# A gated mix of two long convolutions: the short filter as matmuls on a transposed load, and Q rows made for two blocks at a time

## The chip, the core and the metric

The kernel runs on one core of one Trainium2 chip. The metric is the device time of one execution in microseconds. Three runs of the kernel before took 285.6, 288.29 and 289.53 us, so its time is the median, 288.29 us. One more execution was profiled; its span, from the first to the last recorded instruction, is 282.3 us.

## What is computed

There are L = 2048 time steps, D = 448 channels and N = 256 modes per channel. All inputs are bf16, and `A_ref` and `B_ref` are the two convolution branches.

```python
# A: the kernel of the convolution is a sum over the modes of a channel
dt = exp(log_dt)[:, None]; A = A_re + 1j*A_im; Bc = B_re + 1j*B_im; Cc = C_re + 1j*C_im
P = exp((dt*A)[:, :, None] * arange(L))
K = einsum("dn,dnl,dn->dl", Cc, P, dt*Bc).real
y_a = causal_conv(u, K) + u * Dskip              # the reference uses FFTs of length 2L
# B: a short filter over k, then a long convolution
k_shift[t] = sum(k[t - 3 + i] * shift_k[:, i] for i in range(4))   # zeros before t = 0
kv = k_shift * v
y_b = u * (causal_conv(kv, ssm_k) + kv * ssm_D)
# mix
g = sigmoid((u * gate_w).sum(-1, keepdims=True))
out = g * y_a + (1 - g) * y_b
```

## The kernel before

**Layout.** Time is split as 32 x 64 and the channels into four groups of 112. A tile such as `vt` or `uu` holds 128 partitions (group g at 32g, the coarse time a on the 32 partitions within it) by 64 fine steps b by 112 channels. The 448 channels are worked in four chunks H of 28 columns (NQG, NC), which are 112 channels of the four groups.

**Convolution by matmuls.** Both sides of a convolution are brought into the frequency domain by two steps: `spread` (L311, psum tiles `ps_c`, matrix `Wc`) and `transform` (L323, `ps`, `s_W`). ACT evacuates both into tiles `zs` (inputs) or `zsK` (the generated K). `swapped` (L703) makes a copy `zsS` with the real and the imaginary half exchanged, by two DMAs from SP. `products` (L385) multiplies by the other side on DVE. Then come `stage_a` (L360, `ps_a`, matrix `sa_R`, evacuated into `U`) and `stage_b` (L373, `ps_b`, matrix `sb_G`), whose results an epilogue multiplies by u and gathers in `ug`.

**K generated in blocks.** K is made in eight blocks j (two to a chunk H) by `KGen` (L392). `Tables.levels` (L576) makes the powers of the modes for a chunk, two blocks at once: phases `ks_ph` on DVE, sines and exponentials on ACT into `ET`. In a block DVE builds 25 complex Q rows (`kg_TQ`, two buffers, M = 112 modes wide) and 32 P rows (`kg_TP`): `mult` makes products into `kg_P`, `add` sums them, and `leaf` writes products that need no sum (rows 17 to 24). Then PE runs 224 small matmuls `pk`: 25 columns of `kg_TQ` as weights, a strided view of `kg_TP` as the moving side. ACT evacuates `pk` into `kg_S`; `gather` (L475) sorts it by matmuls (`ps_g`) into `kg_KT`, which is spread with `WcK` into `zsK`, in groups of 4, 4, 3 and 3 columns, or 7 and 7 for the last two blocks. `step` (L893) ties a block j to the stages of one convolution, in the order of `seq`.

**The short filter.** 16 DMAs on SP load k into `kt` (L720), in pieces of 112 KB whose rows are 224 bytes. One shifting matmul (`ps_h`) fills the three steps before each row of 64. For eight fine steps at a time (L758 to 768) DVE multiplies a window of k by the four taps (`kvt`, 3584 elements), eight matmuls with the identity add the four products up (`ps_v`), and ACT evacuates into `kt`. Four DVE products with `vt` give `kv`.

**Set-up.** Six loads bring the modes (224 KB each). `wide` transposes them on PE (`ps_m`, 48 pieces), and `scaled` (L526) multiplies by dt on DVE. `Consts.stage_b` (L234) makes G by 16 sines on ACT with a mask in the scale (`sb_G`).

**Order.** Every call is recorded by the class `Order` (L132) and issued in the order of the list `ORDER` (L41), which fixes the order on each engine; the tile framework adds the semaphores and the pools make an instruction wait for its buffer. PSUM has three tiles of two banks (`psum`), one for `pk`, and one for `ps_g`; `qp` has NBQ = 8 buffers. All instructions are issued from L144, so that the profile's rows name this one line, and a reader goes by the names of the tiles.

Of the kernel before, what the change touches and what calls it, by code (L numbers as in the profile page):

```python
# [17 lines left out]
P = 128  # L18
# [13 lines left out]
NQ = 25  # L32
# [5 lines left out]
NBQ = 8  # L38
# [3 lines left out]
    "604 2 1 188 173 582 190 160 194 73 186 19 0 174 192 187 74 534 22 576 5 189 75 593 526 583 9 525 11 3 606 177 4 "  # L42
    "30 26 25 23 67 528 552 161 536 550 18 8 21 597 544 166 16 49 32 198 175 171 542 69 33 191 38 76 535 176 13 529 "
    "196 172 577 537 179 543 580 602 178 12 162 195 181-182 527 193 553 197 65 15 163 201 184 545 588 594 183 589-590 "
    "202 72 20 6 46 24 540 14 70 31 29 538 532 34 27-28 35 37 36 40 44 42 51 66 39 41 45 79 180 541 539 531 77 "
    "234-241 52 43 50 47-48 199 56 68 242 78 164 168 595 100-108 533 215-222 603 200 167 591 581 185 530 90 109 592 "
    "120-128 598 110-118 546 129 548 547 223 551 150 224 140 130 225-232 169 233 203-204 119 151-159 549 243-260 557 "
    "556 554 131-139 555 503 80 205-212 599 165 17 10 7 499 213 474 170 478 494 482 214 517 262 507 578 516 584 513 "
    "481 585 493 476 498 469 477 486 512 508 141-149 91-98 475 99 468 267 285-301 471-473 261 81-89 55 54 53 367 "
    "364-365 487 319-326 366 489 502 327 268-283 302-317 284 318 607 490 263 600 346-354 495 504 518 264 505 837-844 "  # L50
    "421-428 519 479 586 509 500 62 61 63 514 337-345 265 596 587 601 501 491 579 488 483-484 506 515 1124 1126 "
    "370-386 429 558 521 564-565 266 520 1127 570 845 560 64 608-635 574-575 71 636-663 522 1129 523 510 524 480 1131 "
    "496 1137 563 485 566 664-719 470 720 803-818 1133 571 567 561 721-722 819 1138 492 1135 497 568 573 511 404-420 "
    "1113 387-402 1114-1115 1140 1116 1142 1109 2488 569 562 1117 1122 1119 1118 57 59 786-801 1110 559 802 572 "
    "820-836 2492 2491 355-362 1852 1121 403 430-437 2494 363 457-464 328-335 438 465 336 439-446 2497 1108 60 58 "
    "448-455 1111-1112 2489 447 1464-1479 1498-1513 2503 1480 2496 456 1851 1123 1853 1143 1125 1854 1128 1855 723 "
    "1130 1856 1132 2514 1859 1120 1134 605 777-784 2490 1141 1136 2515 1514-1522 1139 1144-1175 2495 1523 1860 2502 "
    "2504 1857-1858 2516 726-741 368 1272-1303 1861 1176-1207 785 742 760-776 2510 1862 743-758 960-967 2519-2520 759 "
    "2521 369 466 1208-1239 2511 467 1863 969-976 2512-2513 968 977 1304-1367 1240-1271 1368 2508 2507 2498 1864-1865 "
    "2499 2517 933-941 1867 2509 863-879 725 1869 2523 2505 1369-1386 2500 1481-1496 2524-2525 1871 2501 1866 1497 "  # L60
    "2542 2533-2534 2543 1868 1873 2544 1879 880-896 2535 2506 906-914 1644-1651 846-861 1387-1426 1652 2518 1427 "
    "915-931 862 932 2537-2538 2545 1875 1878 2539 1876 1880 2562-2563 2529 1870 2564 1872 2526 1874 2528 2565 1877 "
    "1881 897-905 942-949 1847 1461 1446-1451 1662-1670 950 2530 2557 1452 1075-1106 2551 2566 3331 2531-2532 "
    "978-1074 2554 1671-1679 2558 2553 2546 2074-2105 1882-1913 2567 2536 2570 1107 2572 2568 2540 1946-1977 1848 "
    "2547 1849 2219-2234 2559 2571 2550 2235 2493 2522 2569 2574 1453-1459 2010-2041 951-959 1653-1660 2552 2549 2541 "
    "2548 1978-2009 1460 1463 2555 2561 2527 2573 2202-2217 1437-1445 1846 1850 2966-2981 2042-2073 2982 2556 2560 "
    "1914-1945 1661 3332 2218 2575 1428-1436 2106 3968 2236-2252 3974 2576 3333 1462 1584-1600 1618-1633 3971 "
    "1635-1642 2107-2123 1643 3975 3977 3970 2124 1634 1601-1616 1524-1540 2125-2164 1575-1582 2165 3334 1583 1617 "
    "3976 1541-1556 2175-2183 3969 2253-2261 1557-1574 3973 2349-2356 2578 3335 2580 2577 2949-2964 1716-1747 2357 "
    "3338 3982 2579 3972 2582 2586 3983 2584 2587 2581 3336 2583 2590 2965 3339 2589 3340 2591 3341 2585 3343 2592 "  # L70
    "1698-1706 3337 3346 2588 1748-1779 3995 3348 2184-2189 1680-1687 3984 1780 3342 3350 3985 3352 2190 2593-2624 "
    "1707-1714 1688 2657-2688 1715 3994 3354 4008 3357 2785-2816 4009 6194 1689-1697 2199 2625-2656 2166-2174 "
    "2322-2330 4010 2340-2347 2198 2200-2201 2983-2998 2191-2197 2753-2784 2999 2721-2752 3000-3008 3996 2689-2720 "
    "2920-2928 3344 3978 3156-3164 2929-2936 3345 3988 3347 3979-3980 3349 3987 3351 3989 2262-2277 4022 2937 2278 "
    "4004 3981 4011 4003 4023 3355 2348 3353 4005 1813-1844 2331-2338 4024 3358 3999 4025 4006 4017 4043 2339 "
    "2313-2320 1781-1812 2321 2817 4012 3986 3060-3068 4018-4019 4000 3356 1845 3991 2818-2834 3990 4042 3360 4044 "
    "4001 3138-3146 2835 2296-2311 3992 2312 4002 4045 4013-4014 2279-2294 4020 2295 3043-3059 4015 2836-2875 3993 "
    "4046 2876 3997-3998 3359 3361 4032 4027 2390-2421 2423-2454 4047 4016 4048 4034-4035 4031 4028 4037 2358-2389 "
    "4050 4049 2422 3426-3457 4052 4051 4007 4053 4041 4021 3554-3585 4030 4033 4038 3490-3521 2895-2900 4040 "
    "2938-2946 4026 2901 2455-2486 3458-3489 3394-3425 2487 4029 4036 4054 3522-3553 3733-3740 3362-3393 2911-2918 "  # L80
    "4055 4039 3741 4057 3699-3714 2902-2907 2919 3009-3024 2908 3715 3025 2886-2894 5388 4056 5393 3026-3042 4059 "
    "4058 4812 4060 4811 4061 4813 4063 4062 4066 4064 5402 4069 3147-3155 3716-3732 5391 3586 2877-2885 5392 "
    "4070-4071 4067 2909-2910 2947-2948 4814 5396 3682-3697 3183-3190 3698 5399 4815 4065 3587-3604 4446-4461 4816 "
    "4072 3174-3181 3605-3644 3191 4819 4462 5394 3645 4068 3192-3200 5395 3646-3653 3182 3129-3137 5389 3120-3127 "
    "5390 3654 3128 4820 5398 5400 3103-3119 4821 5403 4822 5404 4823 5411 5410 5412 3811-3819 4073-4104 4265-4296 "
    "3802-3810 4233-4264 4826 4818 4817 5415 5414 5413 5420 4828 4137-4168 3655-3663 5416 3069-3084 5401 4830 "
    "4169-4232 4105-4136 5419 4297 4825 3165-3173 3671-3677 4824 4832 5421 4827 4834 4829 5407-5409 3664-3669 3085 "
    "3670 4831 5443 5442 4833 4837 3086-3102 5424 5423 4835 724 5445 5444 4749-4765 4400-4408 5422 5437 5425 "
    "4463-4479 4391-4398 4838 4399 3201-3232 4316-4356 4418-4426 5438 5463 4836 3829-3837 4840 4839 5429 5428 5430 "
    "5405-5406 4298-4315 5439 4841 5426 5434 5417-5418 5433 5435 5431-5432 5462 3678-3679 3681 3680 5464 3820-3828 "  # L90
    "4390 4480-4487 4389 5427 5460 5473 4488 3233-3264 5002-5033 4874-4905 4938-4969 4906-4937 4842-4873 3298-3329 "
    "3266-3297 3330 4970-5001 5034-5065 5456 5449 5448 3265 5465 5458 3793-3800 4366-4373 5397 3801 3742-3758 5447 "
    "4715-4731 5459 4409-4417 3776-3792 3759-3774 4374 3775 4732-4748 4357-4364 4766-4774 5436 5466 6200 5467 5476 "
    "5850 5470 5849 5471-5472 5475 5474 5851 5450 5440-5441 4427-4428 5468 5478 5477 5480 4365 5479 3838-3902 5446 "
    "5486 5481 4775-4783 4429-4445 4540-4548 5487 5483 5469 4375-4381 5454 4506-4521 5461 5457 5066 3903-3934 "
    "4382-4388 4523-4538 5455 4522 5067-5084 5452 4539 5451 5453 5852 3935-3967 4558-4565 5085-5125 4489-4505 "
    "4802-4809 5482 5853 5484-5485 5489 5151-5157 5490-5491 4566 5488 5492-5556 5589-5620 5854 5144-5150 6197 "
    "5857-5859 4576-4583 4810 5685-5716 5653-5684 5126-5134 4567-4575 5557-5588 5621-5652 5717 4584 5855 5860 5856 "
    "5861 5863-5864 5862 5866 5865 5868 5867 5870 5869 5873 5871 5874 5876 5135-5142 4549-4556 5143 5872 5878 4557 "
    "5158 5877 5879 4585-4649 5160-5168 4784-4791 5718-5735 5178-5185 4792 5186 5159 5169-5176 5736-5776 5177 "  # L100
    "4682-4713 4650-4681 4714 5875 5187-5197 5792-5805 4793-4801 5808 5806 5777-5791 5880-5975 6203 5807 6198 6195 "
# [894 lines left out]
```

## Time and profile before

| | us |
|---|---|
| runs | 285.6, 288.29, 289.53 |
| span of the profiled execution | 282.3 |
| the profiled execution's own time around its span | not given by the profile |
| end of the first kg_S evacuation | 83.8 |
| end of the last kg_S evacuation | 250.8 |

A row of a group names line, engine, operation, output and inputs with their shape and count; behind the bar stand the busy time of all in us and the mean of one in ns, and behind the second bar the idle time of the engine just before them and what ended it. A piece of the timeline has its start, its length and how many instructions it holds. "PEld" are the weight loads of PE. The clock in a row of windows is the share of full speed that was granted to PE. In the slices of the page a digit is the busy share of 1/40 of the span in tenths.

### The profile page before, as it was taken

What the parts mean: (1) busy time and instruction counts of PE and PEld (TensorE: products, weight loads), DVE (VectorE), ACT (ScalarE), POOL (GpSimd) and SP (SyncE); (2) the same over time, 40 slices, a digit from 0 to 9 for tenths busy, and PEclk for the clock granted to TensorE, in tenths of its full rate; (3) what the DMA queues carried; (4) which work ended last, traced back from release to release, by engine and by line L of the source; (5) the groups of instructions that cost most, each with busy time, mean ns of one, the idle gap of its engine ahead of it and who ended that gap; (6) DMA issues with size and microseconds to landing.
All of it is one profiled execution on the core that took longest, in us unless ns stands there. A gap on an engine that the chain in (4) does not pass through costs nothing.

```text
span 282.3 us, 12050 instructions
## 1 busy us (share of the span) xinstructions
PE 213.7 (76%) x5387; PEld 185.9 (66%) x5387; DVE 261.8 (93%) x540; ACT 250.8 (89%) x409; POOL 12.0 (4%) x43
## 2 busy tenths in 40 slices
PE   0187673776697869888889898879899999979730
PEld 0044243776586768877779787868789887869730
DVE  8999999999999997999999999999968999987950
ACT  5999999999999999999999999999979999948500
POOL 8005000001000001000000000000000000000000
PEclk9999797565888997999999997988979999979995
DMA  6999997590501360240000070015050003430068
GB/s 116 190 182 176 158 168 105 187 175 6 135 2 19 69 115 10 73 107 2 5 2 5 6 181 0 5 22 114 9 128 2 2 5 73 112 88 5 2 126 138
DMA packets 53380, 21.34 MB, mean 76 GB/s; under 512 B 48720, under 2 KB 51664, under 8 KB 53328
## 3 DMA queue, kind: packets, MB, share of 16 engines
q1 hardware_dynamic: 48768, 19.42, 37.2%
q10 hardware_dynamic: 4560, 1.15, 2.2%
q8 instruction: 42, 0.69, 1.1%
q14 instruction: 10, 0.08, 0.1%
HBM read 10.01 MB, written 3.21 MB: 47 GB/s over the span
## 4 chain that ended last, share of the span: by engine, by line
ACT 34%; DVE 30%; PE 21%; issue 5%; DMA 3%; SPq 2%; DVEq 0%
ACT zs L144 11%; PE pk L144 8%; ACT ET L144 8%; DVE kg_P L144 7%; DVE kg_TP L144 5%; PE ps_b L144 4%; ACT zsK L144 4%; ACT U L144 4%; DVE zsS L144 3%; PE ps_c L144 3%; PE ps_a L144 3%; DVE kg_TQ L144 3%; DVE zs L144 2%; DVE kvt L144 2%; DVE ks_ph L144 2%
## 5 line engine op out<-in xcount | busy, mean ns | idle before, releaser
L144 ACT CAST zs<-ps 128x896 bf16<-128x896 f32 x48 | 44.0, 940 | 0.8 <-PE ps L144 0.7
L144 ACT CAST zs<-ps_c 128x1024 bf16<-128x1024 f32 (+1 forms) x48 | 43.4, 933 | 0.0
L144 PE MATMUL pk<-kg_TP,kg_TQ 128*25 128x32 bf16 x1792 | 33.8, 239 | 8.8 <-issue 6.6
L144 PEld LDWEIGHTS <-s_W 128*128 128x128 bf16 x544 | 31.0, 105 | 12.1 <-issue 8.7
L144 PEld LDWEIGHTS <-kg_TQ 128*25 128x25 bf16 x1792 | 28.6, 128 | 12.2 <-issue 8.2
L144 PE MATMUL ps_a<-sa_R,zs 128*128 128x128 bf16 x224 | 34.1, 239 | 3.0 <-ACT zs L144 1.3
L144 DVE TENSOR_TENSOR kg_P<-kg_TQ,ET 128x896 bf16<-128x896 bf16 (+2 forms) x56 | 35.9, 654 | 0.0
L144 PE MATMUL ps<-zs,s_W 128*128 128x112 bf16 x384 | 29.3, 231 | 7.3 <-ACT zs L144 6.2
L144 PE MATMUL ps_a<-sa_R,zsS 128*128 128x128 bf16 x224 | 33.7, 239 | 1.2 <-DVE zsS L144 1.2
L144 PEld LDWEIGHTS <-zsS 128*128 128x128 bf16 x224 | 30.1, 153 | 4.9 <-issue 3.0
L144 ACT CAST U<-ps_a 128x1024 bf16<-128x1024 f32 (+2 forms) x30 | 28.6, 959 | 5.0 <-PE ps_a L144 5.0
L144 PE MATMUL ps_b<-U,sb_G 128*128 128x28 bf16 x1024 | 28.8, 174 | 3.4 <-DVE U L144 1.2
L144 PEld LDWEIGHTS <-zs 128*128 128x128 bf16 x224 | 30.2, 152 | 1.3 <-issue 0.3
L144 PEld LDWEIGHTS <-sb_G 128*128 128x128 bf16 x1024 | 27.8, 96 | 4.3 <-issue 2.3
L144 DVE TENSOR_TENSOR kg_P<-kg_TP,ET 128x1792 bf16<-128x1792 bf16 (+1 forms) x32 | 30.6, 969 | 0.0
L144 DVE TENSOR_TENSOR kg_TQ<-kg_P 128x448 bf16<-128x448 bf16 (+2 forms) x56 | 23.1, 419 | 0.0
L144 PEld LDWEIGHTS <-scratch 128*128 128x128 bf16 x65 | 6.8, 109 | 24.6 <-issue 19.7
L144 ACT ACTIVATE ET<-ks_ph 128x448 bf16<-128x448 int16 x40 | 22.5, 604 | 0.0
L144 ACT CAST zsK<-ps_c 128x384 bf16<-128x384 f32 (+2 forms) x27 | 21.3, 797 | 0.6 <-PE ps_c L144 0.6
L144 DVE TENSOR_TENSOR kg_TP<-kg_P 128x896 bf16<-128x896 bf16 (+2 forms) x40 | 19.7, 503 | 0.2 <-PE pk L144 0.2
L144 PE MATMUL ps_c<-Wc,kv 128*64 128x128 bf16 x224 | 16.6, 303 | 3.9 <-ACT zs L144 3.6
L144 PE MATMUL ps_v<-kvt,scratch 128*128 128x448 bf16 x64 | 16.1, 405 | 4.0 <-ACT kt L144 3.2
(103 smaller groups left out, 463.3 us busy)
## 6 DMA issues: line engine op xcount, KB each, us to landing
zsS<-zs SPq DMA_DIRECT2D x16, 448.0 KB, 5.7
kt<-in_B_k_dram SPq DMA_DIRECT2D x16, 112.0 KB, 4.0
skraw<-in_B_ssm_k_dram SPq DMA_DIRECT2D x16, 112.0 KB, 5.0
vt<-in_B_v_dram SPq DMA_DIRECT2D x4, 448.0 KB, 7.7
uu<-in_A_u_dram SPq DMA_DIRECT2D x4, 448.0 KB, 8.8
xfd<-ks_hold SPq DMA_DIRECT2D x2, 672.0 KB, 3.2
ks_xf<-xfd SPq DMA_DIRECT2D x3, 336.0 KB, 3.7
out_dram<-ug SPq DMA_DIRECT2D x8, 112.0 KB, 4.0
```

Source lines behind the costliest of these rows:

```text
L144: ins = f(*args, **kw)
```

## The change

- **Filter.** k is loaded by four transposed DMAs on SP, 128 channels by 2048 steps each (512 KB, rows of 256 bytes), into `kt[g]`; three of them lie in the buffer of `uu`, so that the loads of u wait for the end of the filter. ACT makes 16 diagonal matrices `diag` of the taps. For each fine step, tap and group one matmul (1024 in all) takes 32 columns of `kt[g]`, 64 steps apart, as weights and a diagonal as the moving side; four taps add up in PSUM. ACT evacuates eight `ps_v` tiles into `kf`, and four DVE products multiply `vt` by them in place; `ug` now is `vt`.
- **Q rows.** They are made once for two blocks, 224 wide, at even j: ten summed rows and 22 unsummed, 32 instead of 25. `kg_TQ` has one buffer instead of two. The tables are split into EQ (both blocks side by side) and EP. The weights of `pk` have 32 columns.
- **Step size.** A diagonal matrix of dt per group takes the place of the identity in 32 of the 48 `ps_m` matmuls, and the DVE products by dt go; ACT copies the results (`early`).
- **G.** Four plain sines on ACT, and 16 DVE products by the mask.
- **Rest.** Columns go in groups of 4, 4, 4, 2 and of 8, 6. The gate is an exponential, an addition and a reciprocal in place of a tanh. NBQ is 6. pk is no longer cleared. `seq` has another order, with stages a and b of the last B chunk beside block 7. The list `ORDER` is new throughout: of the filter, all 1024 matmuls follow the `ps_m` ones in one run, ahead of the first spreads.

```diff
-NQ = 25
+NQ = 32
+NSUM = 10
-NBQ = 8
+NBQ = 6
...
+            nc.scalar.activation(v, low16(both[:, 0:1024]), ACT.Sin, scale=PHASE)
             for g in range(4):
-                nc.scalar.activation(G[:, b0:b0 + 16, :, g, :].rearrange("p b r a -> p (b r) a"),
-                                     low16(ph[:].rearrange("p b r a -> p (b r a)")).rearrange("p (c a) -> p c a", a=32), ACT.Sin, scale=mask[:, g:g + 1])
+                nc.vector.tensor_scalar(out=G[:, b0:b0 + 16, :, g, :].rearrange("p b r a -> p (b r) a"), in0=v.rearrange("p (c a) -> p c a", a=32),
+                                        scalar1=mask[:, g:g + 1], scalar2=None, op0=ALU.mult)
...
+    def q_rows(self):
+        V, EQ, W = self.nc.vector, self.EQ, 2 * M
+        TQ = self.TQ = self.pool.tile([P, NQ, 2, W], bf16, name="kg_TQ", tag="kg_TQ")
...
+        q4 = mult(EQ[:, 0:2].unsqueeze(1), 4)
+        V.tensor_copy(TQ[:, 0], EQ[:, 0:2])
+        add(1, q4)
+        add(2, mult(TQ[:, 0:2], 2))
+        q256 = mult(TQ[:, 0:2], 256)
+        leaf(10, TQ[:, 0:4], 1)
+        add(4, q256)
+        leaf(18, TQ[:, 2:4], 256)
+        add(6, mult(TQ[:, 0:5:4], 512))
+        leaf(22, TQ[:, 1:6:4], 512)
+        add(8, mult(TQ[:, 6:7], 512))
+        add(9, mult(TQ[:, 8:9], 512))
+        leaf(26, TQ[:, 8:10], 256)
+        leaf(30, TQ[:, 9:10], 512)
...
-                                         lhsT=TQ[:, :, c, m], rhs=rhs, start=(hf == 0 and c == 0),
+                                         lhsT=TQ[:, :, c, at + m], rhs=rhs, start=(hf == 0 and c == 0),
...
+                if timed:
+                    nc.tensor.matmul(o, lhsT=x, rhs=self.dt[:, g], start=True, stop=True)
+                else:
+                    nc.tensor.transpose(out=o, in_=x, identity=self.ident[0:112, 0:112])
...
-    for b0 in (48, 32, 16, 0):
-        for g in range(4):
-            nc.sync.dma_start(kt[g * 32:(g + 1) * 32, 3 + b0:19 + b0, :], k4[g][:, b0:b0 + 16, :])
+    for g in range(4):
+        nc.sync.dma_start_transpose(kt[g][:, 16:2064].unsqueeze(1), B_k[0][:, top(g):top(g) + P])
...
+            nc.scalar.mul(diag[:, g, t], ident[:, 0:112] if g < 3 else late, wf[:, 4 * g + t:4 * g + t + 1])
...
+            for i in range(8):
+                for t in range(4):
+                    for g in range(4):
+                        nc.tensor.matmul(pt[32 * g:32 * g + 32, i // 4, (i % 4) * 112:(i % 4 + 1) * 112], lhsT=kt[g][:, 16 + b1 + b0 + i - t:2001 + b1 + b0 + i - t:64], rhs=diag[:, g, t],
+                                         start=(t == 0), stop=(t == 3), tile_position=(0, 32 * g))
...
-    seq = [("B", 0), ("B", 1), ("B", 2), ("A", 0), ("B", 3), ("A", 1), ("A", 2), ("A", 3)]
+    seq = [("B", 0), ("B", 1), ("A", 0), ("B", 2), ("A", 1), None, ("A", 2), ("B", 3)]
```

## The prediction

> **What bounds the kernel now.** First the page's busy lines and slices: whether one engine sets the time.
>
> ```profile
> span 282.3 us, 12050 instructions
> PE 213.7 (76%) x5387; PEld 185.9 (66%) x5387; DVE 261.8 (93%) x540; ACT 250.8 (89%) x409; POOL 12.0 (4%) x43
> ...
> DVE  8999999999999997999999999999968999987950
> ACT  5999999999999999999999999999979999948500
> ```
>
> Two engines are full at once, DVE and ACT, from start until the last eighth. So a gain needs both to lose work, and the smaller loss counts. The chain's shares agree:
>
> ```profile
> ACT 34%; DVE 30%; PE 21%; issue 5%; DMA 3%; SPq 2%; DVEq 0%
> ```
>
> Second, the windows, cut at the steps of the work: set-up with the k filter to 45, to the first kg_S (83.8), the blocks to the end of the last kg_S (250.8), and the tail. Columns: us, busy time and instructions of PE, PEld, DVE, ACT, POOL, granted clock, DMA share, GB/s.
>
> ```profile
> 0.00:16.00 16.00, 2.68 (x14) 1.62 (x15) 15.08 (x66) 12.88 (x14) 5.70 (x39) 1.00 0.91 156
> 16.00:45.00 29.00, 20.82 (x180) 11.75 (x178) 28.64 (x47) 28.78 (x39) 3.99 (x1) 0.94 1.21 170
> 45.00:84.00 39.00, 27.44 (x628) 24.87 (x626) 38.74 (x89) 38.94 (x75) 0.72 (x2) 0.69 0.44 99
> 84.00:250.80 166.80, 144.59 (x4078) 130.46 (x4077) 161.08 (x316) 158.76 (x270) 1.59 (x1) 0.95 0.22 49
> 250.80:282.30 31.50, 18.23 (x495) 17.16 (x493) 18.24 (x27) 11.46 (x15) 0.00 (x0) 0.83 0.34 61
> ```
>
> Up to 250.8 DVE is busy 243.5 us (97%) and ACT 239.4 (ACT idle: 11.4); then comes a chain of 31.5 us. Span = work of the fuller engine up to the last kg_S + its idle time + tail.
>
> Third, the groups and pieces of PE's timeline, for prices:
>
> ```profile
> L144 DVE TENSOR_TENSOR kvt<-kt,scratch 128x3584 bf16<-128x3584 bf16 x8 | 16.0, 2007 | 0.0
> ...
> L144 DVE TENSOR_TENSOR kg_P<-kg_TQ,ET 128x896 bf16<-128x896 bf16 x40 | 24.5, 621 | 0.0
> ...
> L144 DVE TENSOR_TENSOR kg_P<-kg_TP,ET 128x1792 bf16<-128x1792 bf16 x24 | 25.6, 1086 | 0.0
> ...
> L144 DVE TENSOR_SCALAR sa_R<-sa_R 128x256 bf16<-128x256 bf16 x1 | 0.2, 207 | 0.0
> ...
> L144 DVE TENSOR_SCALAR s_ph<-scratch 128x1024 int32<-128x1024 int32 x4 | 3.2, 801 | 0.0
> ...
> L144 ACT ACTIVATE sb_G<-sb_ph,scratch 128x1024 bf16<-128x1024 int16 x16 | 17.5, 1148 | 0.0
> ...
> L144 ACT CAST zsK<-ps_c 128x384 bf16<-128x384 f32 x12 | 10.5, 873 | 0.3 <-PE ps_c L144 0.3
> ...
> L144 ACT CAST zsK<-ps_c 128x512 bf16<-128x512 f32 x12 | 7.4, 618 | 0.3 <-PE ps_c L144 0.3
> ...
> L144 PE MATMUL ps_v<-kvt,scratch 128*128 128x448 bf16 x64 | 16.1, 405 | 4.0 <-ACT kt L144 3.2 <-DVE ks_hold L144 0.5 <-DVE kvt L144 0.3
> ```
>
> ```profile
> 99.91 1.63 PE L144 MATMUL pk<-kg_TP,kg_TQ 128*25 128x32 bf16 x96
> 101.47 1.17 PE L144 MATMUL ps_c<-Wc,uu 128*64 128x128 bf16 x16
> ```
>
> Means overlap: all means times counts make 306.4 us on DVE for 261.8 busy over 540 instructions, so the next starts 0.083 before an end; on ACT 300.8 for 250.8 over 409, 0.12. Prices below are means less these. A smaller 384-element zsK evacuation costs more than a 512-element one: the three-wide output is the slow form.
>
> **DVE, part by part.**
> Filter: the eight kvt multiplies go: 8 x 1.924 = -15.4. The four products with v stay (1792 elements).
> Q rows: by the rows of 224 elements (0.186), 448 (0.302), 896 (0.537), 1792 (1.003) and the 224 copy (0.13), a block makes 2 x 0.186 + 0.13 + 5 x 0.302 + 9 x 0.537 + 1.003 = 7.85. After, a pair of blocks makes 3 x 0.302 + 13 x 0.537 + 5 x 1.003 + a copy of 448 (0.19, between 0.13 and 0.302) = 13.1. 8 x 7.85 - 4 x 13.1 = -10.4: fewer additions, and less start-up per element.
> Step size: four f32 products from PSUM (0.52) and four of prod (0.54) become four differences of 448 (0.54) and four small diagonals; two 1792 combinations (1.0) go too: -3.6.
> G: 16 mask multiplies are new, with no row of their size and form. Nearest are sa_R (256 elements, 0.124 less overlap, so about 0.34 at 1024 if copies scale like the products) and s_ph (0.72 at 1024, int32): 5.4 to 11.5. I take 5.4, since sa_R is the same operation in bf16. Small edits (pk's memset, gate, ident): -0.3.
> Sum -24.3: DVE 261.8 to 237.5 (243.6 with the s_ph price).
>
> **ACT.** G: sixteen scaled sines (1.03) become four plain ones: -12.4. Sixteen diag scalings of 112 elements are new: nearest row the 224-element exponential (0.28); 0.2 each, +3.2 (2.5 to 4.5). Coefficients: four early copies of 448 (0.42) and two f32 ks_b against bf16 ones: +1.7; wt and halo copies go, -0.9, dt's exponential shrinks, -0.4. Widths 4,4,3,3 to 4,4,4,2: -2.7; 7,7 to 8,6: -1.1. One table load more: +1.3. The eight filter evacuations stay. Sum -11.3: 250.8 to 239.5. Before the last kg_S the order list now leaves 7.3 us of ACT for the tail instead of 11.5, so 232.1 there against 239.4: -7.3. DVE has about 216 there against 243.5. ACT is now alone in front, with DVE some 16 us behind.
>
> **PE.** 64 matmuls of 448 columns go (-16.1). 1024 of 112 columns come, in 256 groups of four that share the columns of the array. The nearest four-fold row is pk's: 96 in 1.63 us is 17 ns apiece, 68 a group (58 to 62 between starts), with strided weights and moving side. ps_g, 112 columns moving and contiguous weights, has 49 to 50. I take 62: 15.9 us; strided weights as in the u spreads (16 in 1.17 us; 118 ns between the starts of a pair of 64 columns, 1.84 a column, so 59 for 32) still fit. If weights and moving side added up, 59 + 49 = 108: 27.6 us. pk's weights grow from 25 to 32 columns at twice the stride: 1.84 x 32 = 59, within the 58 to 62, so nothing; up to +8 us on 1792 matmuls if all scales by 32/25, on an engine with 68 us free. [...]
> [...]
>
> **Waits and moves.** SP: 16 k loads go, four transposed loads of 512 KB come behind the modes, whose 224 KB each need about 1.4 us at the 156 to 170 GB/s of the first windows. 3.47 MB in all at 163 is 21 us, so the last lands at 23. That assumes that a transposed load moves like a plain one; no row shows one. Bounds: at 190 (the best slice) 20; at uu's 8.8 us for 448 KB one after another, 10 us each, 48. I take 23, since plain kt rows (4.0 us for 112 KB) overlap each other. Needed: ACT's list ahead of the first kf evacuation sums to 23.9 us (16 diag 3.2, 3 table loads 3.9, 19 exponentials 5.3, 8 phase sines 3.8, s_W 1.8, two 1024 sines 2.1, copies 3.6, rest 0.2); from 2.7 with 2 us of waits it gets there at 28.6. A tile takes 32 groups, 2 us; so landing up to 26 is free. All eight tiles at 2.1 us and ACT's 16.9 us between first and last kf put the last at 46.3.
> Behind: DVE's vt products wait for kf; DVE's list reaches them at 35, so it idles 10 us, inside its 16. PE's skraw and v spreads, queued behind the filter, start some 8 us later than before (zs 38 to 46); uu loads wait for the filter too, but are first spread in step 2. The single TQ buffer: between an odd block's last TP write and the next TQ write DVE has 7 us of other work, while 224 pk matmuls need 3.8. SP's ks_xf and uu stand behind the table saves, which wait for the tables; 672 KB lands in 3.2. NBQ of 6 and the group widths cost nothing that I can place. The B3 stages moved behind block 7 fill the tail's idle PE: ps_a pieces of 1.8, 2.6 and 0.7 us stood in the chain of waits between 250 and 256.4, ahead of the gather; of these 5.1 I take 3.5, since one half of KA remains: tail 28.
>
> **Sum.** 232.1 + ACT idle (11.4 as before + 2) + tail 28 = 273.5 span against 282.3. The page has no outer time for its execution; the median of three runs (285.6, 288.29, 289.53) is 6.0 above the span, kept: 279.5 us, -3%.
>
> **Rivals.**
> A. Late transposed loads, the one that ends slower. The filter is the first work that needs all four; beyond 26 us each us is a us of ACT's chain. Even with before at landing 35 (279.5 + 9), over 2% slower from 41, 301.5 at 48. For: uu's 8.8, and small packets (256 B runs). Against: the kt rows. [...]
> B. Filter groups at 108: 27.6 us, ending at 51 instead of 46, ACT held 5.5: 285. Against: pk's 62.
> C. Three engines within 10% of each other hand waits around: PE 213, DVE 237, ACT 239. ACT's idle 11.4 doubles where TQ, NBQ or the zsS swaps meet: 285 to 291; beyond 294 only with 14 us more. For: waits already spread thinly over ps, ps_c, ps_a (5 to 6 us each). Against: DVE's new slack.
> D. DVE's slack also takes ACT's idle time down to 3 to 5: 270 to 274.
>
> **Chances.** Forecast 0.47 (275 to 282.5), D 0.07, B 0.09, C 0.20 (0.14 within 2%), A 0.17 (0.04 within 2%, 0.13 beyond). Faster by over 2% (under 282.5): 0.54; within: 0.27; slower (over 294): 0.19. Two per cent is about what a measurement of this kernel can tell. The range 271 to 299 leaves out the end of D and the far end of A, 0.15.
>
> **What would show it.** ACT busy 239, DVE 238; kvt gone; masks 0.34 apiece; Q pair 13.1; a filter group 62 ns; ACT not waiting at the first kf (else landing after 26); DVE waiting 10 us at vt for kf; last kg_S 245, tail 28. Wrong if PE waits for kt beyond 26, if ACT idles over 20 before the last kg_S, or masks cost over 0.7.

## The result, and the profile after

The changed kernel took 301.62 us (median of four runs, 297.24 to 303.37) against 287.69 for the kernel before (four runs, 285.6 to 289.53). The ratio is 1.041, with a 95% interval of 1.029 to 1.053. Forecast were 279.5 us and a range of 271 to 299: the change went the other way. The ratios leave out runs over 1.5% above the fastest of their kernel, the profiled one of after (303.37 us) among them, while the times are medians of all runs. So the two need not agree, and differences of 2 us against the parts of that profile prove little. Its span is 301.5 us, so 1.9 us lie around a span (2.2 to 2.4 in later runs of before), and not the 6.0 that the sum had taken.

The busy lines of the page, as they were shown of before, and the shares of the chain of work that ended last:

```profile
span 301.5 us, 13923 instructions
PE 223.1 (74%) x6346; PEld 203.1 (67%) x6346; DVE 246.1 (82%) x491; ACT 243.9 (81%) x416; POOL 8.3 (3%) x44
...
PE 46%; ACT 27%; DVE 12%; issue 7%; DMA 4%; SPq 0%; DVEq 0%; ACTq 0%
```

DVE lost 15.7 us of busy time and ACT 6.9, and the span grew by 19.2. PE, 21% of the chain before, is 46% of it now. The windows of after are cut where the long run of the filter's matmuls begins (29.0), at the end of the last kf evacuation (61.2, cut at 61.3), of the first kg_S (97.4), of block 5's kg_S (231.2) and of the last (270.4). The columns are those of the prediction.

```profile
0.00:29.00 29.00, 6.30 (x62) 5.05 (x63) 20.65 (x83) 18.99 (x47) 5.13 (x33) 1.00 0.64 144
29.00:61.30 32.30, 21.41 (x1036) 20.03 (x1035) 20.01 (x58) 25.01 (x45) 1.28 (x8) 0.89 0.59 108
61.30:97.40 36.10, 31.36 (x709) 27.61 (x709) 32.79 (x61) 34.41 (x49) 0.91 (x2) 0.95 0.68 105
97.40:231.20 133.80, 115.70 (x3161) 106.72 (x3160) 124.23 (x229) 128.90 (x222) 0.94 (x1) 0.94 0.22 46
231.20:270.40 39.20, 32.59 (x949) 29.09 (x949) 33.31 (x41) 28.33 (x49) 0.00 (x0) 0.83 0.22 50
270.40:301.50 31.10, 15.67 (x441) 14.61 (x437) 15.10 (x24) 8.22 (x13) 0.00 (x0) 0.81 0.33 61
```

The same cuts in the kernel before (the last evacuation of its filter ended at 40.7):

```profile
0.00:40.70 40.70, 21.22 (x153) 11.35 (x154) 39.48 (x106) 37.39 (x46) 9.68 (x40) 0.96 1.10 164
40.70:83.80 43.10, 29.52 (x665) 26.75 (x665) 42.78 (x92) 43.02 (x81) 0.72 (x2) 0.72 0.52 107
83.80:222.60 138.80, 120.10 (x3171) 108.48 (x3170) 133.29 (x276) 135.19 (x237) 1.59 (x1) 0.94 0.21 45
222.60:250.80 28.20, 24.68 (x913) 22.11 (x912) 27.99 (x42) 23.77 (x35) 0.00 (x0) 0.99 0.30 69
```

Two stretches are longer: up to the end of the filter (61.3 against 40.7) and the last two blocks (39.2 against 28.2). Between them after gains 12 us (169.9 against 181.9), partly because work was put off to the last two blocks (ACT works 28.3 us there against 23.8). In the first two windows ACT is busy 44.0 of 61.3 us: it waits 17.3. The waits of after (engine and tile that waits, releaser, then total us, times and the longest):

```profile
PE ps_v L151 <- issue: 10.6, 7, 2.5
...
PE ps_v L151 <- ACT diag L151: 8.4, 2, 6.1
DVE vt L151 <- ACT kf L151: 8.1, 2, 6.2
ACT kf L151 <- PE ps_v L151: 7.3, 5, 3.5
ACT kg_S L151 <- PE pk L151: 6.2, 3, 2.9
...
ACT ks_mag L151 <- DVE early L151: 3.8, 1, 3.8
```

The first line is the new one. "issue" says that PE waited for nothing that the profile shows. PE's timeline in the filter (start, length, count, in brackets the idle time before):

```profile
29.07 3.98 PE L151 MATMUL ps_v<-diag,kt 128*32 128x112 bf16 x161 [2.24 <-ACT diag L151]
33.33 2.34 PE L151 MATMUL ps_v<-diag,kt 128*32 128x112 bf16 x128 [0.28 <-issue]
37.88 2.28 PE L151 MATMUL ps_v<-diag,kt 128*32 128x112 bf16 x128 [2.21 <-issue]
42.71 2.70 PE L151 MATMUL ps_v<-diag,kt 128*32 128x112 bf16 x128 [2.54 <-issue]
47.53 3.21 PE L151 MATMUL ps_v<-diag,kt 128*32 128x112 bf16 x128 [2.12 <-issue]
51.26 2.26 PE L151 MATMUL ps_v<-diag,kt 128*32 128x112 bf16 x128 [0.52 <-issue]
55.27 2.26 PE L151 MATMUL ps_v<-diag,kt 128*32 128x112 bf16 x128 [1.74 <-issue]
58.72 1.58 PE L151 MATMUL ps_v<-diag,kt 128*32 128x112 bf16 x81 [1.19 <-issue]
```

Five of these holes, 9.8 us, stand in the chain of work that ended last. Every piece between two holes marked "issue" is 128 matmuls, and with their 128 weight loads 256 instructions. That number belongs to PE's program, and not to the filter, whose tile has 128 matmuls too but whose pieces do not start with a tile (5, 9 and 161 come first, so the first hole is after 175). The page lists a queue 8 of the kind "instruction"; the first fence is before, the second after (packets, MB, share):

```profile
q8 instruction: 42, 0.69, 1.1%
```

```profile
q8 instruction: 49, 0.80, 1.2%
```

All of these packets have 16,384 bytes. The 42 of before come to 64 bytes for each of its 10,774 PE instructions (matmuls and weight loads); if they carry PE's program, a packet is 256 instructions, the number in a piece. The experiments below bear that out: 576 pairs fewer in the wide filter took away 4 packets (49 to 45), and 896 pairs fewer in half of pk took away 7, in a version of after (45 to 38) as in before (42 to 35). In after's filter the transfer records show one packet per 3.5 to 4.8 us, each 0.9 to 1.6 us long. It starts 1.1 to 2.0 us after PE has resumed, and PE resumes 1.3 to 1.6 us after its end. PE runs a piece of 256 instructions in 2.3 us (3.2 at half clock) and then stands. Bulk loads ran beside the filter (DMA share 0.59), but the packets of the blocks, with a share of 0.22, took about as long (0.9 to 1.4 us), and in before and after no packet started less than 3.4 us after the one ahead of it.

### The profile page after: what moved, and what is told of

Same layout as the page of the kernel before. It is cut to its first block, busy times and chain, and to the rows that moved or that the text cites. A ratio compares the mean times of both kernels' runs of the same rounds, so it can differ in the third digit from the quotient of the medians.

```text
span 301.5 us, 13923 instructions
## 1 busy us (share of the span) xinstructions
PE 223.1 (74%) x6346; PEld 203.1 (67%) x6346; DVE 246.1 (82%) x491; ACT 243.9 (81%) x416; POOL 8.3 (3%) x44
## 4 chain that ended last, share of the span: by engine, by line
PE 46%; ACT 27%; DVE 12%; issue 7%; DMA 4%; SPq 0%; DVEq 0%; ACTq 0%
ACT zs L151 10%; PE pk L151 8%; PE ps_c L151 8%; PE ps_a L151 8%; PE ps_v L151 7%; PE ps_b L151 6%; PE ps L151 5%; ACT U L151 4%; ACT ET L151 4%; ACT zsK L151 3%; DMA zsS<-zs 2%; PE ps_g L151 2%; DVE kg_TP L151 2%; ACT L151 2%; DVE kg_P L151 2%
## 5 line engine op out<-in xcount | busy, mean ns | idle before, releaser
L151 PE MATMUL pk<-kg_TP,kg_TQ 128*32 128x32 bf16 x1792 | 34.6, 242 | 4.0 <-issue 3.9
L151 PE MATMUL ps_v<-diag,kt 128*32 128x112 bf16 x1024 | 21.4, 253 | 20.3 <-issue 10.6
L151 PEld LDWEIGHTS <-kg_TQ 128*32 128x32 bf16 x1792 | 31.7, 160 | 6.4 <-issue 5.1
L151 PE MATMUL ps_b<-U,sb_G 128*128 128x28 bf16 x1024 | 31.6, 175 | 5.8 <-issue 3.0
L151 PE MATMUL ps_a<-sa_R,zs 128*128 128x128 bf16 x224 | 34.7, 246 | 0.6 <-ACT U L151 0.4
L151 PEld LDWEIGHTS <-sb_G 128*128 128x128 bf16 x1024 | 29.0, 96 | 8.8 <-issue 5.8
L151 PE MATMUL ps<-zs,s_W 128*128 128x112 bf16 x384 | 28.6, 226 | 8.5 <-ACT zs L151 7.5
L151 PEld LDWEIGHTS <-kt 128*32 128x32 bf16 x1024 | 19.8, 155 | 22.0 <-issue 22.0
L151 ACT CAST U<-ps_a 128x1024 bf16<-128x1024 f32 (+1 forms) x30 | 27.2, 922 | 5.6 <-PE ps_a L151 5.5
L151 DVE TENSOR_TENSOR kg_TQ<-kg_TQ,ET 128x896 bf16<-128x896 bf16 (+1 forms) x36 | 24.7, 722 | 0.1
L151 DVE TENSOR_TENSOR kg_TP<-kg_TP,ET 128x1792 bf16<-128x1792 bf16 x16 | 17.4, 1088 | 1.6 <-ACT ET L151 1.2
L151 PE MATMUL ps_c<-Wc,uu 128*64 128x128 bf16 x224 | 17.0, 289 | 2.2 <-ACT zs L151 1.4
```

What stands on the lines that cost most here:

```text
L151: ins = f(*args, **kw)
```

## The experiments

Theory 1: the filter's 1024 pairs of small instructions outrun the supply of PE's program; the cost is in their number, not in their columns. Rivals: the columns (PE's own work), or the diagonals that come late. The first four kernels were measured together, with before at 285.66 us.

**Narrow matmuls.** Same count; taps 1 to 3 move 28 columns.

```diff
-rhs=diag[:, g, t]
+rhs=diag[:, g, t, 0:28 if t else 112]
```

> The 1024 filter matmuls stay, but taps 1 to 3 move only 28 of the 112 columns (the other channels of these taps are left out): 196 columns for a time step instead of 448. Theory 1 (PE waits for its own program: about 4.3 us for every 128 pairs of weight load and matmul, whatever they do): the filter takes 30 to 31 us as before, with the same 1 to 2.5 us holes every 128 pairs, last kf near 60, total unchanged (297 to 303). Theory 2 (weight loads and moving columns add up in the array, 59 + 49 ns a group): a group falls to about 80 ns, the filter to 23 to 25 us, total 6 us less. Theory 3 (late transposed loads): the first matmul waits for kt; the stretch itself follows theory 2.

Measured: 301.93 us in a single run, span 300.2. PE's timeline of this kernel:

```profile
33.08 2.16 PE L150 MATMUL ps_v<-diag,kt 128*32 128x28 bf16 x128 [1.57 <-issue]
37.63 2.19 PE L150 MATMUL ps_v<-diag,kt 128*32 128x28 bf16 x128 [2.39 <-issue]
42.18 2.26 PE L150 MATMUL ps_v<-diag,kt 128*32 128x28 bf16 x128 [2.36 <-issue]
```

The pieces start 4.5 us apart, as the first ones of after do, with holes of 1.6 to 2.4 us that no engine causes. With over half of the columns gone the filter's matmuls still end at 59.7 (60.3 in after), so the columns are not its cost. The granted clock is 0.67 over the filter (28.7 to 59.6; it falls to half at 39.0), and the six pieces of 128 take 2.16 to 2.27 us, ahead of 39.0 (the first row) and behind it (the third) alike. So with 28 columns not even a piece's pace comes from the columns.

**Diagonals first.** In ORDER alone, the 16 `nc.scalar.mul(diag...)` go in one run.

```diff
-... 71 ... (the other 15 spread over ACT's list)
+... 71-86 ...
```

> Only the order on ACT changes: all 16 diagonals are made in one run at 9 us. Theory 1: the first filter matmul still waits for its PSUM buffer (19.9), but the two waits for diag (8.4 us) go; 8 stretches of 4.3 us end near 54 instead of 60; total 6 us less, about 295, ratio to the kernel before 1.02. Theory 3: no change, since kt would then hold the filter until 29.

Measured: ratio 1.040 [1.032, 1.048], 297.11 us, span 293.3. The waits for diag are gone, the holes marked "issue" still add up to 7.4 us, and the last kf ends at 57.7 instead of 61.2. So late diagonals cost 3.5 us there; in the ratio of the whole (1.041 for after) that does not show. PE's waits for ACT now fall at other places, and the first holes marked "issue" stand where they did, after 175 matmuls (32 + 143) and 128 later:

```profile
23.92 3.58 PE L151 MATMUL ps_v<-diag,kt 128*32 128x112 bf16 x143 [1.70 <-ACT early L151]
27.86 1.37 PE L151 MATMUL ps_v<-diag,kt 128*32 128x112 bf16 x49 [0.36 <-issue]
29.83 1.43 PE L151 MATMUL ps_v<-diag,kt 128*32 128x112 bf16 x79 [0.60 <-ACT early L151]
32.96 2.12 PE L151 MATMUL ps_v<-diag,kt 128*32 128x112 bf16 x81 [1.70 <-issue]
```

**Wide matmuls.** 448 matmuls for 1024: one matmul serves several fine steps, by a run of diagonals as the moving side. The sum is the same and the diagonals come as late as in after.

```python
for n in (0, -3, -2, -1, 1, 2, 3):
    lo, hi, s = max(n, 0), min(n + 4, 4), 16 + b1 + b0 + 4 * i + n
    for g in range(4):
        nc.tensor.matmul(pt[32 * g:32 * g + 32, i, lo * 112:hi * 112], lhsT=kt[g][:, s:s + 1985:64],
                         rhs=diag[:, g, lo - n:hi - n, :], start=(n == 0), stop=(n == 3), tile_position=(0, 32 * g))
```

> The same filter with the same weights and columns in all, but one matmul moves up to four neighbouring taps (336 columns on average 256): 448 matmuls instead of 1024, diag made as late as in the changed kernel. Theory 1: 896 instructions are 3.5 blocks of program, 15 to 17 us; last kf near 47 instead of 60; total 12 to 13 us less, 288 to 290, ratio about 1.00. Theory 2 with all columns and weights adding up: 19 us. Theory 3: no change of the start.

Measured: ratio 1.029 [1.021, 1.037], 293.73 us. PE's timeline of this kernel:

```profile
36.78 1.80 PE L148 MATMUL ps_v<-diag,kt 128*32 128x448 bf16 x56 [1.38 <-ACT kf L148]
39.85 3.36 PE L148 MATMUL ps_v<-diag,kt 128*32 128x448 bf16 x112 [1.27 <-ACT kf L148]
44.43 1.79 PE L148 MATMUL ps_v<-diag,kt 128*32 128x448 bf16 x56 [1.21 <-ACT kf L148]
47.92 1.81 PE L148 MATMUL ps_v<-diag,kt 128*32 128x448 bf16 x56 [1.70 <-ACT kf L148]
```

No hole is marked "issue" any more. A tile takes 1.8 us and PE waits for ACT instead. The last kf ends at 53.5: 7.7 us of the set-up come back by fewer instructions alone. With the narrow run, which left the number and took the columns, this shows theory 1 for the filter. It is not the whole of the loss: 47 and a ratio about 1.00 were expected, and the ratio went from 1.041 to 1.029 only, with intervals that overlap.

**Both.** Wide matmuls and diagonals first.

> Both edits: 448 filter matmuls, and the diagonals first. Theory 1: the filter runs from 20 to about 37, then ACT's own list sets the last kf near 45; total 16 us less than the changed kernel, about 285, ratio 0.98 to 0.99. If the changed kernel is bound elsewhere (rival C, waits in the block stage), the gain stays near 8 and the ratio near 1.02.

Measured: ratio 1.019 [1.007, 1.031], 293.24 us; the last kf at 53.8 and not at 45. The diagonals on time are worth nothing more at the filter's end once the matmuls are wide: ACT reaches the first kf at 36.1 (35.9 in "wide"). In the total the intervals of the two overlap. The forecast of this run was missed, so something else holds ACT.

**Coefficients ahead.** The wait of ACT's `ks_mag` for DVE's writes into `early` (3.8 us in after, 4.7 in "both") is taken away, by moving two of those writes behind the exponentials that still read the tile (on top of "both").

```diff
-... write early (hold 0), write early (hold 0), coefficients of hold 1 ...
+... coefficients of hold 1, (exponentials), write early (hold 0), write early (hold 0) ...
```

> Third edit to the set-up of the changed kernel, after the wide filter and the early diagonals: the four DVE writes of the coefficients into the table of dt*A come later in the order, so that ACT's exponentials of that table no longer stand behind DVE's products (one wait of 4.7 us in the profile of e4). Theory 4 (what is left of the set-up's loss is ACT's own waits): first kf 4 to 5 us earlier (31 to 32), last kf near 49, total 4 us less, about 289, ratio 1.00 to 1.01. Rival: the wait only moves to the next instruction that needs the coefficients; first kf stays at 36.

Measured: ratio 1.021 [1.016, 1.026], 291.99 us. The first kf begins at 35.0, 1.1 us earlier than in "both", where 4 to 5 were expected. The wait moved to the next instructions of the list (2.1 us for ps_m, 1.95 for early).

**Half of pk.** To see whether PE's pk, now 32 columns wide, holds the blocks, half of its matmuls are left out, in "coefficients ahead" and in the kernel before.

```diff
-for c in range(2):
+for c in range(1):
```

> As e5, but each block runs 112 of its 224 pk matmuls (the imaginary half of the sum over the modes is left out): 896 pairs and 3.5 blocks of program less on PE, nothing else changed. Theory 5 (in the blocks PE with its program stream now ends the waits; ACT's idle time there, 12 to 16 us against 8 before, is waiting for PE): kg_S waits for pk (6 us) go, ACT's idle time in the blocks falls under 6 us, total 7 to 10 us less than e5. Rival (ACT's waits are a chain through ACT and DVE themselves, PE is only in it): 0 to 3 us.

> Control for e6: the kernel before, with the same half of pk left out. There DVE and ACT are both at 95 to 97% up to the last kg_S, and ACT waits 0.2 us for pk: 2 to 4 us less, ratio 0.985 to 0.99. If it gains as much as e6, PE binds both kernels alike and theory 5 does not explain the difference.

Measured: 287.47 us, ratio 1.007 [1.004, 1.011]; and before 278.84, ratio 0.977 [0.974, 0.980]. The first gains 4.5 us, the second 6.5. ACT's idle time from the first kg_S to the last went from 13.7 to 8.0, and in before from 8.0 to 1.7. (The 896 pairs left out are 7 packets, and not the 3.5 of the expectation.) So the wider pk is not what sets the two apart. That theory falls, and with it the reading of before that only DVE and ACT bound it: taking work from PE alone made it 2.3% faster, more than the 2 to 4 us expected. The blocks of that kernel (166.8 us in before) show both other engines at 99%:

```profile
84.40:243.80 159.40, 132.61 (x3288) 119.54 (x3286) 157.69 (x313) 157.71 (x270) 2.39 (x1) 0.93 0.22 49
```

**DVE's load.** 16 us of DVE work more in the blocks (two products of 1792 elements in each), then 15 to 16 us less (the `back` half of the P rows left out), the latter also in before.

```diff
+for _ in range(2):
+    V.tensor_tensor(out=self.dummy[:], in0=self.dummy[:], in1=self.dummy[:], op=ALU.mult)
```

> As e5, with two products of 1792 elements more on DVE behind the last kg_TP write of each block: 8 x 2 x 1.0 = 16 us of DVE work that nobody waits for. If DVE's saved time is slack, as forecast (ACT alone in front): 0 to 4 us more than e5. If DVE still ends the waits in the blocks: 10 to 16 us more.

> As e5, without the upper 16 P rows (the two products of 1792 elements in each block are left out and pk reads the lower rows twice): 16 us of DVE work less, PE and ACT as before. Theory 6 (DVE's saving was taken in the set-up, where DVE waits, and in the blocks DVE still ends the waits, as 16 us more cost 9): 6 to 10 us less, ratio 0.99 to 1.00. If DVE is only one of three and the waits go round, 2 to 4 us.

> Control for e10: the kernel before without the upper P rows, 16 us of DVE work less. ACT is at 95% there up to the last kg_S and idle 11 us, so 4 to 8 us less, ratio 0.975 to 0.985; if it gains the same as e10, DVE's part in the end is the same in both kernels.

Measured: with more 300.89 us, ratio 1.054 [1.050, 1.058], 8.9 us above "coefficients ahead". With less 293.77, ratio 1.024 [1.014, 1.033], no gain over its 1.021, where 6 to 10 us or 2 to 4 were expected. Before with less 285.8, ratio 0.994 [0.989, 1.000], where 4 to 8 us were expected. The blocks of that last kernel, first kg_S to last kg_S:

```profile
84.20:250.80 166.60, 143.34 (x4086) 129.61 (x4085) 150.26 (x304) 158.64 (x270) 0.39 (x1) 0.95 0.22 49
```

DVE does 11 us less there than before (161.1), and the stretch is 166.6 us long against 166.8. DVE was 97% busy in before and taking work from it alone bought nothing there, as ACT kept its work (158.6 us after 158.8); but in "coefficients ahead" DVE stands so close to the bound that 16 us more cost 9.

**Diagonals on DVE.** If ACT's own list bounds the set-up, taking the 16 scalings off it must shorten it (on top of "coefficients ahead").

```diff
-nc.scalar.mul(diag[:, g, t], ident[:, 0:112] if g < 3 else late, wf[:, 4 * g + t:4 * g + t + 1])
+V.tensor_scalar(out=diag[:, g, t], in0=..., scalar1=wf[:, 4 * g + t:4 * g + t + 1], scalar2=None, op0=ALU.mult)
```

> As e5, with the 16 diagonals of the filter made by DVE (which idles 12 us before the last kf) and not by ACT (which is the fuller engine there, 4.5 us for them). Theory 4 (ACT's list sets the end of the set-up): first kg_S 3 to 4 us earlier (85), total 3 to 4 us less, ratio about 1.01. If the set-up hangs on something else (DVE's coefficients, the modes), the idle time of ACT grows by what is saved: 0 to 1 us.

Measured: ratio 1.018 [1.011, 1.026], 291.11 us. Up to the last kf ACT works 4.4 us less and idles 3.4 us more, and the first kg_S ends 1.0 us earlier. ACT's waits for ps_m grew from 2.3 us to 7.2, and it still waits 1.9 for early. So in the set-up ACT waits for a chain through PE and DVE (modes, ps_m, early), and not for room in its own list.

**Fillers for the clock.** In blocks 6 and 7 the granted clock is 0.83 (before 0.99). Idle-filling matmuls into a spare corner of pk's tile were to keep it up, on the author's guess, which no run shows, that a busier PE is granted more: 61 of them between 200 and 243 us, 185 over the whole, 223 in before.

```diff
+nc.tensor.matmul(pk[:, 448:512], lhsT=R[:, 0:128], rhs=R[:, 128:192], start=True, stop=True)
```

> As e5, with 61 matmuls of 128 x 64 more that compute nothing (into unused columns of pk's bank), put where PE stands still between 200 and 243 us in the profile of e5. There PE works only when ACT lets it, its granted clock then falls to 0.5 for 14 us, and blocks 6 and 7 take 37.7 us against 28.2 before, although all engines have as much work. Theory 7 (the low clock in blocks 6 and 7 is what costs there): the clock stays up, PE's busy time in these blocks falls from 32 to 26 us, total 4 to 6 us less than e5, ratio 1.00. Rival (these blocks are long because of the order of their work, the clock is a symptom): 0 to 2 us less or some more, since the added matmuls cost 4 us of PE.

> As e12, with 185 such matmuls wherever PE stands still in e5 between 60 and 262 us and no sum in pk's bank is open. Theory 7: the granted clock goes from 0.92 towards 0.97, total 5 to 8 us less than e5. Rival: no gain, 0 to 4 us more.

> Control: 223 such matmuls in the kernel before, where PE stands still between 44 and 252 us. Before, the low clock lies in the set-up (45 to 69 us), where ACT and DVE are 99% busy and PE is not waited for, so -2 to +2 us; the more it gains, the less e13 says of the change.

Measured: ratios 1.019 [1.013, 1.026], 1.013 [1.000, 1.026] and 1.014 [1.006, 1.023] (the last in before, where fillers cost). The clock in blocks 6 and 7 did not change: what it was short of full, times the length of these blocks, comes to 6.6 and 6.8 us against 6.9 without fillers. So the runs say nothing on what a full clock would bring, and that theory is untested. Nor do the other variants with the same blocks settle it: 6.2 us short go with blocks 38.7 us long ("diagonals first"), 6.9 with 37.8 ("coefficients ahead") and 9.7 with 40.0 ("diagonals on DVE").

**What is left.** None of the versions of after beats the kernel before, and "half of pk", the nearest, leaves out a part of the result. The windows of "coefficients ahead", the best understood of them, for a ledger against before:

```profile
0.00:52.70 52.70, 24.79 (x520) 21.40 (x521) 40.37 (x140) 43.35 (x90) 7.23 (x41) 0.93 0.77 154
52.70:88.70 36.00, 31.74 (x709) 28.42 (x709) 32.81 (x61) 34.38 (x49) 1.21 (x2) 0.92 0.62 91
88.70:221.50 132.80, 115.09 (x3161) 105.48 (x3160) 124.51 (x228) 128.81 (x222) 0.39 (x1) 0.97 0.21 47
221.50:259.20 37.70, 32.02 (x937) 28.91 (x937) 33.20 (x40) 28.02 (x47) 0.00 (x0) 0.82 0.23 52
```

Up to the last kg_S ACT works 234.6 us (before 239.4: 4.8 saved) and idles 24.6 (before 11.4: 13.2 lost), so that kg_S comes 8.4 us later. Of the idle time 9.3 lie ahead of the last kf, 1.6 up to the first kg_S, 4.0 up to block 5 and 9.7 in blocks 6 and 7 (before 3.3, 0.1, 3.6 and 4.4). At block 5 the two kernels are level (221.5 and 222.6), partly because work was put off: of the 9.5 us by which blocks 6 and 7 are longer (37.7 against 28.2), 4.2 are work of ACT that stood earlier before (28.0 us there against 23.8), and 5.3 are idle time. In blocks 6 and 7 of this kernel ACT waits for PE:

```profile
ACT kg_S L148 <- PE pk L148: 5.2, 2, 3.1
ACT kg_KT L148 <- PE ps_g L148: 2.4, 1, 2.4
ACT U L148 <- PE ps_a L148: 1.6, 2, 1.0
```

PE is busy 32.0 us there against 24.7, with nearly the same number of matmuls (937 and 913), and its granted clock is 0.82 against 0.99. The 7.3 us more are about the 6.9 us by which the clock was short of full; that points to the clock, but does not show it. Whether the low clock or the new order, with stages of the last B chunk in these blocks, makes the 5.3 us of idle time stays open: the two were not separated, and moving those stages back was not tried. Open too is how to win back the 6.0 us of idle time that the mended set-up has more than before ahead of the last kf: its waits are named above, and no run took them away.

## Why the prediction was wrong

**The prices held.** The durations of all DVE instructions add up to 277.9 us after 306.4, or 28.5 less; the sum, freed of its overlap, had 28.4 (24.3, and 0.083 for each of the 49 instructions fewer). Three rows of after with terms of the sum, the mask, the products of a Q pair and pk:

```profile
L151 DVE TENSOR_SCALAR sb_G<-sb_ph,scratch 128x1024 bf16<-128x1024 bf16 x16 | 7.3, 479 | 4.2 <-ACT sb_ph L151 4.2
L151 DVE TENSOR_TENSOR kg_P<-kg_TQ,ET 128x1792 bf16<-128x1792 bf16 x12 | 13.0, 1088 | 0.3
L151 PE MATMUL pk<-kg_TP,kg_TQ 128*32 128x32 bf16 x1792 | 34.6, 242 | 4.0 <-issue 3.9
```

A mask is 479 ns, 0.40 less overlap, where 0.34 was taken (7.3 us in all against 5.4). pk costs 242 ns with 32 columns of weights after 239 with 25, as said. But DVE's busy time fell by 15.7 only, because fewer instructions overlap the one ahead of them: 386 of 491 begin before its end, and in before 517 of 540. The 131 overlaps fewer are, at 0.083, 10.9 of the 12.8 us. "Means less these" held only while DVE was full (93% busy in before, 82% in after).

**"I take 62: 15.9 us", and "all eight tiles at 2.1 us", failed.** The pace inside a piece is right: 32 groups in 2.3 us, 64 to 67 ns a group from start to start, and 92 (3.2 us a piece) at half clock. Rival B's 108 is refuted. What failed is that a piece ends after 128 matmuls. The matmuls run from 29.1 to 60.3, 31 us for 16, and last kf ended at 61.2 instead of 46.3. Two lines of before had the sign: the chain, shown in the prediction, has "issue 5%", and the waits have

```profile
PE pk L144 <- issue: 6.6, 6, 2.4
```

Neither was given a price. In after the holes of the filter are seven and come to 10.6 us, and fewer instructions won back 7.7 us of the set-up ("wide").

**"It gets there at 28.6" failed.** ACT reached its first kf at 35.7. Its work ahead of that is 26.1 us for the 23.9 listed, its idle time 9.6 (the start included) for 4.7. The idle time lies in waits for others: 3.85 for early, 1.97 for diag's identity, 0.5 for ps_m. The sum had asked what stands on ACT's list and not what each entry waits for. The diagonals were costed as 3.2 us of ACT's work (5.3 by the row of 376 ns, 4.2 without overlap), and not as something that PE waits for: 8.4 us.

**"ACT idle (11.4 as before + 2)" failed, and is the error in one number:** it came to 34.7, and over 20 was one of the prediction's own signs of being wrong. Against 232.1 + 13.4 + 28 the profile of after has 235.7 + 34.7 + 31.1. Thus 21 of the 28 us between the two spans are waits, 4 are work of ACT, and 3 the tail, which kept its length (31.1 after 31.5) although the B stages left it; why was not looked into. Of the 21 us of waits, 8.0 went with the wide matmuls alone (ACT's idle time up to the last kg_S is 26.7 us there) and 2.1 more with the two changes of order on top (24.6); the cause of the other 11 is only argued or stays open ("What is left"). The 6.0 us around the span, 1.9 in truth, made the forecast 4 us too long, and so hid a part of the error.

**"Two engines are full at once" left out the third.** Both were busy over 95%, and the rule that a gain needs both to lose work fits one control: 15 us less work for DVE alone (6%) brought 0.6% [0.0, 1.2]. It does not fit the other: half of pk's work on PE, with 68 us free, brought 2.3%, out of ACT's idle time in the blocks (8.0 to 1.7 us). "DVE some 16 us behind" was not slack either: 16 us more in "coefficients ahead" cost 8.9. And the stretch of before with the lowest clock, 0.69 from 45 to 84 us, is not PE's busiest: by the prediction's own rows PE was busy 70% of it and 87% of the blocks, which had 0.95. Where engines hand work around, a busy share does not say which one the end waits for.

**The rivals.** A has 301.5 us, close to the result by luck, and its cause did not come: the transposed loads landed 4.1 to 4.7 us after issue, the last of them at 19.7, and the first filter matmul, at 19.9, did not wait for it. D did not come. C has the right kind of cause in the blocks (ACT idles 15.8 there against 8.0) and the versions with a mended filter (291 to 294) lie just above its 285 to 291. The supply of the program, the largest part that an experiment took away, was in none of them. It should have been asked of 2048 instructions in a row on one engine.

## What to carry to other kernels

Count the instructions of a new run of small matmuls as well as their columns: here PE got 256 instructions, weight loads included, per 3.5 to 4.8 us, so a run that executes them in 2.3 us is bound by its number, and a wide form of the same sum was the remedy (no such holes, 7.7 us). A wait marked "issue" in a profile is a cost to be priced like any other. Before two full engines are named as the bound, take some work from each in turn, and from the engine between them, and see what the time does. A busy share alone did not answer it here.

## What was not expected of the hardware

- PE's program came in packets of 16,384 bytes (queue 8: 42 in before, 49 in after). In after's filter each packet began 1.1 to 2.0 us after PE had resumed, and PE resumed again 1.3 to 1.6 us after its end: seven holes, 10.6 us. In before, where the 224 pk matmuls of a block stand among other matmuls, the holes marked "issue" at pk were six and came to 6.6 us.
- Transposed loads of 512 KB landed in 4.1 to 4.7 us (three of the four; the trace has no landing of the first). The plain pieces of 112 KB in before took 4.0 us.
- The granted clock falls to half in stretches of 3.4, 6.8 or 10.2 us in before and after (the last of each record reaches beyond the span): 13.7 of the 39.2 us of blocks 6 and 7 in after. The first such stretch begins at 31.7 us in before, at 44.0 in after and at 39.0 in "narrow". In after's filter the stretch from 44.0 to 50.8 us follows 3.4 us in which PE was busy for 1.3, between holes of the supply; whether the one brings the other about was not shown. Fillers did not lift the clock in blocks 6 and 7, and why is not settled.
- A trace's clock record starts with its first entry, at 18.1 us in before and 33.7 in after, and the windows show 1.00 ahead of it. That is no full clock: the ps_v matmuls of before took 578 ns at 14 to 16 us, 577 in the half-clock stretch at 34 us and 350 at full clock, and the 161 filter matmuls of after from 29.1 to 33.1 us took 92 ns a group, as at half clock.
- Four matmuls that share the array's columns, each with weights over all rows, took 64 to 67 ns a group from start to start with 448 columns in all at full clock, and 62 to 65 with 196 columns at either clock ("narrow"). At half clock the 448 columns took 92. So 196 columns do not set the pace of a group. The prediction's sum of weight loads and columns, 59 + 49, is 108.
